# Small values gathered into one tile, turned values put into free places, and two quarters of a K chunk kept, in a decode kernel of four layers

## The chip, the cores and the metric

The kernel runs on one core of one Trainium2 chip. The metric is device time in microseconds of one launch. Three runs of the kernel before gave 673.77, 673.06 and 672.82 us; the median, 673.06, is the time before.

## The reference

Attention with a cache of 4096 positions and an MLP with GELU stand in turn, two of each, for one token of 512 values:

```python
def _A_ref(x, k_cache, v_cache, wq, wo):
    q = (x @ wq).reshape(B, Sq, H, Dh).transpose(0, 2, 1, 3)      # H = 32, Dh = 128
    scores = jnp.einsum("bhqd,bhkd->bhqk", q, k_cache) * (Dh ** -0.5)   # 4096 keys
    p = _softmax(scores, axis=-1)
    o = jnp.einsum("bhqk,bhkd->bhqd", p, v_cache)
    return o.transpose(0, 2, 1, 3).reshape(B, Sq, H * Dh) @ wo
def _B_ref(x, w1, b1, w2, b2):                                    # 512 -> 1376 -> 512
    return jnp.einsum("bsf,fd->bsd", _gelu(jnp.einsum("bsd,df->bsf", x, w1) + b1), w2) + b2

x = A_x
x = x + _A_ref(_layernorm(x), A_k_cache, A_v_cache, A_wq, A_wo)
x = x + _B_ref(_layernorm(x), B_w1, B_b1, B_w2, B_b2)
x = x + _A_ref(_layernorm(x), A_k_cache, A_v_cache, A_wq, A_wo)   # the same caches and weights
x = x + _B_ref(_layernorm(x), B_w1, B_b1, B_w2, B_b2)
```

All values are float32. One pass over the caches and weights is some 157 MB, far over what the core's memory holds.

## The kernel before

**Two passes.** A pass is one attention layer and its MLP. The 32 heads are taken in eight groups of four. A group's K is one block of 128 partitions by 32 quarters of 512 values (a quarter, `U`, is 256 KB; four are a chunk, 32 a block of 8 MB); its V has the same size. Pass one takes the groups from 0 to 7, pass two from 7 back to 0, so that what the first leaves in the memory serves the second: K of group 7 whole, V of group 7 whole, V of group 6 in part (26 quarters in place and six copied into PSUM tiles `pK`), and of K of group 6 one quarter, copied by ScalarE into `KEPT_K` (line 399).

**The arena.** One large tile holds a ring of three homes of a block each (`A_AT`, `B_AT`, `C_AT`), and behind the third home, from `SHARED` on, places for the MLP's weights, one quarter of scratch (`SCRATCH`), and a `PAIR` of weight blocks, wo of this group and wq of the next. Beside the arena there are tiles of their own: the identity for transposes, `zq` (queries with zeros around them), `x_wide` and `on_wide` (operands of 128 columns and a few more, of which a matmul reads a window), the biases, `ml` and `mb` of the softmax, a tile `smalls` of 160 columns for all small values, and two work buffers, `turned` and `mt`, for transposed values.

**A group.** `scores` multiplies K by a query that stands in a window of `zq`; `exponentials` finds the maximum, turns it into a bias with two small transposes on VectorE (DVE) and lets ScalarE take the exponentials; `weights` transposes them on TensorE (PE) into PSUM `pO` and copies them into a `turned` buffer, and forms the reciprocal sum `rl`. Of V, PE multiplies three chunks of eight; DVE multiplies the other five by the weights and adds them up (`weighted`, lines 239 to 250). These sums and the group's output product come only in the next group, beside its scores (`group`, lines 369 to 381): `sum_up`, `head` (which writes `on_wide`), the scores, `out_product` with windows of `on_wide`, `exponentials`, the turn of the output by four transposes of DVE, and `weights`. The next group's queries are made with windows of `x_wide` (`next_queries`).

**What sets the order.** All loads of weights, K and V go out on one queue (SP, SyncE), in program order; a load whose place is still being read makes all behind it wait. The first input `xcol` and the biases go out on ScalarE's queue. PE's matmuls are kept in program order. Other instructions are ordered by a scheduler at compile time, which also makes every wait from the places that instructions read and write.

**The change of passes** (lines 415 to 484). After the last V chunks come wo, w1 in four loads, and w2 in five (`W2_AT_CHANGE`), each into the places of w1 that have just been read. Behind w2 come wq for the second head group of pass two (when row 3 of w2 is through), K of group 6 in pieces (`begin_k`), into places that become free one after another, and a pair of weight blocks. Meanwhile PE takes the scores of group 7 from K that is there (line 456), its exponentials, the queries of group 6 (line 465), the weights and V of group 7 (line 469). When these values are through, the next K block may be loaded into `A_AT`. `idle` is a matmul with zero weights whose result nobody uses; it fills PE's waits.

Of the kernel before, what the change touches and what calls it, by code (L numbers as in the profile page):

```python
# [22 lines left out]
J = 4  # L23
# [30 lines left out]
def decode_layers(ctx: ExitStack, tc: tile.TileContext, x, k, v, w, w1, b1, w2, b2, out):  # L54
    nc = tc.nc
    const = ctx.enter_context(tc.tile_pool(name="const", bufs=1))
    work = ctx.enter_context(tc.tile_pool(name="work", bufs=1))
# [5 lines left out]
    smalls, places = ctile("smalls", 160), {}  # L63

    def small(name, n=1):
        if name not in places:
            a = sum(b - a for a, b in places.values())
            places[name] = a, a + n
        a, b = places[name]
        assert b <= 160 and b - a == n  # L70
        return smalls[:, a:b]

# [29 lines left out]
    nc.scalar.dma_start(xcol, x)  # L102
    nc.scalar.dma_start(b1c, b1)
    nc.scalar.dma_start(b2c, b2)

    ident = ctile("ident", P)
    make_identity(nc, ident)
    negmean = ctile("negmean", 32)
    nc.vector.memset(negmean, -1.0 / D)
    power = small("power")  # L110
    nc.gpsimd.memset(power, -0.5)

    zero, one = small("zero", 4), small("one")
    nc.vector.memset(zero, 0.0)
    nc.vector.memset(one, 1.0)
# [5 lines left out]
    for t in (pS, pO):  # L121
        nc.vector.memset(t, 0.0)
    zq = ctile("zq", J, 2 * C - 1)
    ml, mb = (ctile(n, 32) for n in ("ml", "mb"))
    for t in (zq, ml, mb):
        nc.vector.memset(t, 0.0)

    def of_32(t, n, i=0):
        return t[:, : 32 * n].rearrange("p (c q) -> p c q", q=32)[:, :, i]


    x_wide, on_wide = ctile("x_wide", 32 * J + 6), ctile("on_wide", 32 * J + 3)
    nc.vector.memset(x_wide, 1.0)
    nc.vector.memset(on_wide, 0.0)

# [5 lines left out]

    def turned(src, wide=False):

        t = work.tile([P, P], F32, name="turned")
        if wide:
            for j in range(J):
                q = slice(32 * j, 32 * j + 32)
                nc.vector.transpose(t[q], src[q, P * j : P * (j + 1)])  # L148
        else:
            nc.vector.transpose(t, src[:, :P])  # L150
        return t
# [16 lines left out]
    def minus_mean(s, at):  # L168
        for j in range(J):
            matmul(at[32 * j : 32 * j + 32, :], negmean, s, start=True, stop=True)  # L170
        return at
# [21 lines left out]

    def queries(to, negm, wide=False):
        qt = turned(to, wide)
        z = zq
        nc.vector.scalar_tensor_tensor(z[:, :, C - 1], of_32(qt, J, 1), negm, of_32(qt, J),
                                       op0=ALU.mult, op1=ALU.add)
        return z

    def scores(z, c, kt):
        for j in range(J):
            matmul(pS[32 * j : 32 * j + C, :], z[:, j, C - 1 - c : 2 * C - 1 - c], kt[j],
                   start=(c == 0), stop=(c == C - 1))

    def exponentials(sc, nsc):
        nc.vector.tensor_reduce(ml[:, 0:1], pS, axis=AX.X, op=ALU.max)  # L207
        mt, m, bias = work.tile([P, 32], F32, name="mt"), small("m"), work.tile([P, 32], F32, name="mt")
        nc.vector.transpose(mt, ml)
        nc.vector.tensor_reduce(m, mt[:, :C], axis=AX.X, op=ALU.max)  # L210
        nc.vector.tensor_scalar(mb[:, :C], m.to_broadcast([P, C]), nsc, None, op0=ALU.mult)
        nc.vector.transpose(bias, mb)  # L212
        p = at(SCRATCH, U)
        nc.scalar.activation(p, pS, AF.Exp, bias=bias[:, 0:1], scale=sc, accum_out=ml[:, 0:1])  # L214
        return p

    def weights(p):
        for b in range(4):
            tc.keep_in_program_order(nc.tensor.transpose(  # L219
                pT[:, b].rearrange("p j r -> p (j r)"), p[:, P * b : P * (b + 1)], ident))  # L220
        pt = work.tile([P, P], F32, name="turned").rearrange("p (c j b) -> p c j b", j=J, c=C)
        nc.vector.tensor_copy(pt, pT[:, :, :, :C].rearrange("p b j c -> p c j b"))  # L222
        lt, l, lr, rl = work.tile([P, 32], F32, name="mt"), small("l"), work.tile([P, 32], F32, name="mt"), small("rl")
        nc.vector.transpose(lt, ml)  # L224
        nc.vector.tensor_reduce(l, lt[:, :C], axis=AX.X, op=ALU.add)
        lb = small("lb", 32)
# [42 lines left out]

    def head_out(rl, wt, last=False):  # L270
        on = head(rl, last)
        to = pS if last else pO
        out_product(on, wt, to, last)
        return of_32(turned(to, wide=not last), 4)

# [9 lines left out]
    def mlp(xs, s, w1_t, w2_t, load_w2=None, behind_w2=None):  # L285
# [107 lines left out]
    for g in range(G):  # L393
# [4 lines left out]
        if g == G - 2:  # L398
            nc.scalar.copy(at(KEPT_K, U), at(k_home + NC * C - U, U))
        if g < G - 2:  # L400
# [14 lines left out]
        if final:  # L415
            wo_t = by_four(load(PAIR, of_w(g % 2, g, 1)))
            for i in range(3):
                load_w1(SHARED, i, i + 1)
            own = head_out(rl, wo_t, last=True)
            load_w1(SHARED, 3, 4)  # L420
        else:
# [3 lines left out]
            z = next_queries(xs, negm, wq_t)  # L425
    x1, s1 = set_x(own, 1.0, acc, queries=False)

    k_t = []
# [125 lines left out]
```

## Time and profile before

| what | value |
|---|---|
| median of three runs | 673.06 us (672.82 to 673.77) |
| the profiled execution's own time | 673.26 us |
| its span from the first to the last instruction | 671.5 us |
| PE, DVE, ScalarE busy, share of the span | 59%, 49%, 3% |
| read from device memory | 285.88 MB, 426 GB/s over the span |
| share of the 16 DMA engines' time, SP's queue | 99.1% |

Rows of the timeline have the start and the length in microseconds, the engine, the line, the operation and its operands (out<-in) with partitions and elements, and how often it came; in brackets stands how long the engine was idle before it and what ended that. SPq and ACTq are the issues of transfers. PEclk, in the busy time by stretches, is the share of TensorE's clock that was granted. Rows of DMA issues give the size in KB and the microseconds from the issue until all has landed; several issues in one row share a median.

### The profile page before, as it was taken

The page shows a single profiled execution, that of the slowest core. Times are in us where ns is not written, and L with a number is a line of the kernel's source. Part 1 is how long each engine was busy: PE and PEld are TensorE (multiplying, and loading weights), DVE is VectorE, ACT ScalarE, POOL GpSimd, SP SyncE. Part 2 cuts the span into 40 slices and gives each one's busy share as a digit, 9 for nine tenths or more (in the row PEclk, how much of TensorE's full clock was granted, in tenths as well). Part 3 has the DMA queues.
Part 4 walks back from the last instruction along what each step waited for, and adds up shares of the span by engine and source line. Part 5 has one row for each costly group of instructions (what it writes and reads, how often), then busy time and mean ns, then how long its engine had stood idle before and what let it go on. Part 6 is the DMA issues. An engine that isn't in the chain of part 4 may idle for free. (4 is left out here: it accounts for less than half of the span.)

```text
span 671.5 us, 5755 instructions
## 1 busy us (share of the span) xinstructions
PE 397.1 (59%) x2458; PEld 107.2 (16%) x2458; DVE 330.9 (49%) x483; ACT 22.5 (3%) x48; POOL 4.4 (1%) x21
## 2 busy tenths in 40 slices
PE   4443753647618456386877878747527466275585
PEld 1100110111202111011213222211102111021122
DVE  2049276393682845930112221294682945927631
ACT  0010000000000000001000110000000000000000
POOL 1000000000000000000000000000000000000000
PEclk9666775976868767677978898978668857687698
DMA  9999999999999999999999999999999999999997
GB/s 375 437 438 434 437 434 437 402 466 437 437 434 401 430 439 437 437 438 423 429 412 403 431 427 432 418 451 438 434 437 409 459 433 427 433 437 413 431 421 299
DMA packets 11545, 286.25 MB, mean 426 GB/s; under 512 B 1792, under 2 KB 1792, under 8 KB 3584
## 3 DMA queue, kind: packets, MB, share of 16 engines
q1 hardware_dynamic: 11088, 285.88, 99.1%
q8 instruction: 19, 0.31, 0.2%
q10 hardware_dynamic: 432, 0.01, 0.0%
q14 instruction: 6, 0.05, 0.0%
HBM read 285.88 MB, written 0.00 MB: 426 GB/s over the span
## 5 line engine op out<-in xcount | busy, mean ns | idle before, releaser
L84 PE MATMUL pS<-arena,zq 128*8 128x512 f32 x1024 | 137.3, 697 | 35.2 <-DMA arena<-in_k 31.4
L243 DVE TENSOR_TENSOR arena<-arena,turned 128x10240 f32<-128x10240 f32 x11 | 119.1, 10826 | 41.8 <-DMA arena<-in_v 41.8
L84 PE MATMUL pO<-arena,turned 128*4 128x512 f32 x584 | 98.1, 832 | 53.5 <-DMA arena<-in_v 51.9
L84 PE MATMUL pO<-arena,smalls 128*4 128x512 f32 (+3 forms) x158 | 30.4, 813 | 133.3 <-DVE arena L248 128.0
L248 DVE TENSOR_TENSOR arena<-arena 128x2048 f32<-128x2048 f32 (+1 forms) x33 | 98.5, 2985 | 0.7
L207 DVE TENSOR_REDUCE ml<-pS 128x1 f32<-128x512 f32 x16 | 11.1, 692 | 152.1 <-PE pS L84 152.1
L84 PEld LDWEIGHTS pS<-arena,zq 128*8 128x8 f32 x1024 | 29.3, 100 | 149.6 <-issue 112.7
L84 PE MATMUL pO<-arena,on_wide 128*128 128x512 f32 (+1 forms) x136 | 49.2, 527 | 4.0 <-DVE on_wide L266 2.7
L84 PE MATMUL pS<-arena,x_wide 128*128 128x512 f32 x88 | 41.0, 608 | 2.4 <-DMA arena<-in_w 2.4
L258 DVE STREAM_TRANSPOSE arena<-pO 128x512 f32<-128x512 f32 x16 | 11.5, 717 | 58.2 <-PE pO L84 58.2
L84 PEld LDWEIGHTS pO<-arena,turned 128*4 128x4 f32 x584 | 16.6, 104 | 119.2 <-issue 115.3
L214 ACT ACTIVATE arena<-pS,mt,smalls 128x512 f32<-128x512 f32 x16 | 12.4, 777 | 493.3 <-DVE mt L212 493.3
L219 PE MATMUL pO<-ident,arena 128*128 128x128 f32 x64 | 10.6, 291 | 30.5 <-DVE turned L148 16.4
L148 DVE STREAM_TRANSPOSE turned<-pO 32x128 f32<-32x128 f32 x64 | 19.8, 309 | 17.8 <-PE pO L84 17.1
L84 PEld LDWEIGHTS pO<-arena,smalls 128*4 128x4 f32 (+2 forms) x158 | 3.1, 88 | 145.1 <-DVE arena L248 137.1
L84 PEld LDWEIGHTS pO<-arena,on_wide 128*128 128x128 f32 (+1 forms) x136 | 19.4, 164 | 34.9 <-issue 28.1
L84 PE MATMUL pO<-arena,x_wide 128*2 128x128 f32 (+1 forms) x88 | 16.2, 396 | 9.6 <-POOL x_wide L162 6.7
L84 PEld LDWEIGHTS pS<-arena,x_wide 128*128 128x128 f32 x88 | 16.1, 193 | 32.6 <-DMA arena<-in_w 16.9
L84 PE MATMUL pS<-arena,smalls 128*1 128x128 f32 (+1 forms) x188 | 14.3, 316 | 2.3 <-DVE smalls L309 1.2
L148 DVE STREAM_TRANSPOSE turned<-pS 32x128 f32<-32x128 f32 x44 | 13.7, 311 | 0.8
L219 PEld LDWEIGHTS pO<-ident,arena 128*128 128x128 f32 x64 | 7.0, 145 | 43.2 <-issue 25.1
L224 DVE STREAM_TRANSPOSE mt<-ml 128x32 f32<-128x32 f32 x16 | 3.4, 212 | 17.0 <-ACT arena L214 17.0
(73 smaller groups left out, 95.6 us busy)
## 6 DMA issues: line engine op xcount, KB each, us to landing
arena<-in_w SPq DMA_DIRECT2D x13, 2048.0 KB, 11.5
arena<-in_k SPq DMA_DIRECT2D x4, 4096.0 KB, 25.3
arena<-in_v SPq DMA_DIRECT2D x2, 4096.0 KB, 39.1
arena<-in_w SPq DMA_DIRECT2D x6, 1024.0 KB, 20.4
arena<-in_v SPq DMA_DIRECT2D x3, 2048.0 KB, 43.3
arena<-in_v SPq DMA_DIRECT2D x1, 6144.0 KB, 29.6
arena<-in_w SPq DMA_DIRECT2D x6, 688.0 KB, 30.6
arena<-in_v SPq DMA_DIRECT2D x4, 1024.0 KB, 46.4
```

The source lines that it names most:

```text
L84: tc.keep_in_program_order(nc.tensor.matmul(*a, **kw))
L148: nc.vector.transpose(t[q], src[q, P * j : P * (j + 1)])
L207: nc.vector.tensor_reduce(ml[:, 0:1], pS, axis=AX.X, op=ALU.max)
L214: nc.scalar.activation(p, pS, AF.Exp, bias=bias[:, 0:1], scale=sc, accum_out=ml[:, 0:1])
L219: tc.keep_in_program_order(nc.tensor.transpose(pT[:, b].rearrange("p j r -> p (j r)"), p[:, P * b : P * (b + 1)], ident))
L224: nc.vector.transpose(lt, ml)
L243: nc.vector.tensor_tensor(t, t, w.unsqueeze(2).to_broadcast([P, 4 * J * (C - BY_PE), P]), op=ALU.mult)
L248: nc.vector.tensor_tensor(a, a, b, op=ALU.add)
L258: nc.vector.transpose(ot, pO)
```

## The change

- All tiles beside the arena become columns of one tile, `cells`: the identity, `zq` (39 columns instead of 60, the four heads' windows overlapping in their zeros), one wide operand in place of two (x in columns 0 to 7 of each 32, the head's output in columns 8 to 11), `ml` and `mb` one column apart, and the values of the GELU, which share columns with `lb` and `mt`. Other small values take the 20 columns that are left free in each 32 of the wide operand, in the order in which they are first asked for: negmean, power, one, the values of the mean and the variance, sc, nsc, the maximum `m` and `l` fill the first; `rl`, `o`, `acc` and `x1` the second. Those that come by DMA (xcol and the two biases) lie behind, outside the wide operand, in columns that DVE fills with zeros first; these two memsets now stand ahead of the three transfers.
- `turned` values have no buffer of their own. They go to a free quarter of the arena (`TURNED`), to `SCRATCH` around the change of passes, once to the identity's place (which is rebuilt by `make_identity` after the first queries of pass two) and once into the home `C_AT`.
- `KEPT_K` holds two quarters; ScalarE's copy moves 1024 columns, and the last piece of K of group 6 is 12 quarters instead of 13.
- The second and third load of w2 at the change are rows 2 to 4 and 4 to 8 instead of 2 to 5 and 5 to 8, and the filler matmul behind row 4 stands behind row 3.
- In the first group of pass two a filler matmul is put behind the scores; the queries of group 6 are multiplied ahead of `exponentials`, and turned between its bias and its ScalarE instruction.
- negmean is one column read with stride 0. The scratch for descriptors is 128 instead of 256 bytes per partition.

```diff
+TURNED = SHARED + 9 * U
-ARENA = KEPT_K + U
+ARENA = KEPT_K + 2 * U
+ZQ = C - 1 + J * C
+WIDE = 32 * J + 8 + 3 + 1
+CELLS = 425
-W2_AT_CHANGE = ((0, 2), (2, 5), (5, 8), (8, 10), (10, 11))
+W2_AT_CHANGE = ((0, 2), (2, 4), (4, 8), (8, 10), (10, 11))
...
+    cells = ctile("cells", CELLS)
+    ident, zq, wide = cells[:, :P], cells[:, P : P + ZQ], cells[:, P + ZQ : P + ZQ + WIDE]
+    x_wide, on_wide = wide, wide[:, 8:]
+    first_small = P + ZQ + WIDE
+    by_dma = ("b1c", "b2c", "xcol")
+    gaps, places = [P + ZQ + 32 * j + 12 for j in range(J)], {}
+    ends = [a + 20 for a in gaps]
...
+            fit = [j for j in range(J) if name not in by_dma and gaps[j] + n <= ends[j]]
...
     wq_t = by_four(load(SHARED, of_w(1, 0, 1)))
-    b1c, b2c = ctile("b1c", FB), ctile("b2c", 4)
-    xcol = ctile("xcol", 4)
+    nc.vector.memset(wide, 1.0)
+    nc.vector.memset(cells[:, first_small:], 0.0)
+    b1c, b2c, xcol = small("b1c", FB), small("b2c", 4), small("xcol", 4)
     nc.scalar.dma_start(xcol, x)
...
+    turned_at = [at(TURNED, P)]
...
-        t = work.tile([P, P], F32, name="turned")
+        t = turned_at[0] if to is None else to
...
-    def exponentials(sc, nsc):
+    def exponentials(sc, nsc, between=None):
...
         nc.vector.transpose(bias, mb)
+        if between:
+            between()
         p = at(SCRATCH, U)
...
-                if c in (4, 7, FB - 1):
-                    idle(pO, U if c == 4 else U // 2)
+                if c in (3, 7, FB - 1):
+                    idle(pO, U if c == 3 else U // 2)
...
-            nc.scalar.copy(at(KEPT_K, U), at(k_home + NC * C - U, U))
+            nc.scalar.copy(at(KEPT_K, 2 * U), at(k_home + NC * C - 2 * U, 2 * U))
...
-            own = head_out(rl, wo_t, last=True)
+            own = head_out(rl, wo_t, last=True, home=ident)
...
+    turned_at[0] = at(SCRATCH, P)
...
     negm, z, sc, nsc = first_queries(xs, s, wq_t)
+    make_identity(nc, ident)
...
-            begin_k(C_AT + 2 * NC, 13)
-            k_t.append(at(KEPT_K, U))
+            begin_k(C_AT + 2 * NC, 12)
+            k_t += [at(KEPT_K, U), at(KEPT_K + U, U)]
     pair = load(C_AT + 24 * U, of_w(g % 2, g - 1, 2))
-    p = exponentials(sc, nsc)
+    idle(pO)
     for c in range(4):
         query_block(c, xs, wq_t)
-    z = queries(pO, negm)
+    p = exponentials(sc, nsc, lambda: queries(pO, negm, to=at(C_AT + 21 * U, P)))
     pt, rl = weights(p)
...
+    turned_at[0] = at(TURNED, P)
```

More of the change, by code (lines that the diff above doesn't have):

```diff
@@ L61, in ctile @@
         return const.tile([P, *shape], F32, name=name)
-    smalls, places = ctile("smalls", 160), {}
+    cells = ctile("cells", CELLS)
+    ident, zq, wide = cells[:, :P], cells[:, P : P + ZQ], cells[:, P + ZQ : P + ZQ + WIDE]
+    x_wide, on_wide = wide, wide[:, 8:]
+    first_small = P + ZQ + WIDE
+    ml, mb = cells[:, first_small : first_small + 32], cells[:, first_small + 1 : first_small + 33]
+    gelu = first_small + 33
+    lb, mt = cells[:, gelu : gelu + 32], cells[:, gelu + 32 : gelu + 64]
+    rest = gelu + 6 * FB
+    by_dma = ("b1c", "b2c", "xcol")
+    gaps, places = [P + ZQ + 32 * j + 12 for j in range(J)], {}
+    ends = [a + 20 for a in gaps]
     def small(name, n=1):
+        nonlocal rest
+        if name.startswith("gelu_"):
+            i = "huaztg".index(name[-1])
+            return cells[:, gelu + FB * i : gelu + FB * (i + 1)]
         if name not in places:
[L67 to L71, printed above, removed]
+            fit = [j for j in range(J) if name not in by_dma and gaps[j] + n <= ends[j]]
+            if fit:
+                places[name] = gaps[fit[0]], n
+                gaps[fit[0]] += n
+            else:
+                places[name] = rest, n
+                rest += n
+        a, m = places[name]
+        assert m == n and rest <= CELLS
+        return cells[:, a : a + n]
     arena = const.tile([P, ARENA], F32, name="arena")
@@ L104, in decode_layers @@
     nc.scalar.dma_start(b2c, b2)
-    ident = ctile("ident", P)
     make_identity(nc, ident)
-    negmean = ctile("negmean", 32)
+    negmean = small("negmean")
     nc.vector.memset(negmean, -1.0 / D)
@@ L111, in decode_layers @@
     nc.gpsimd.memset(power, -0.5)
-    zero, one = small("zero", 4), small("one")
-    nc.vector.memset(zero, 0.0)
+    one = small("one")
     nc.vector.memset(one, 1.0)
@@ L122, in decode_layers @@
         nc.vector.memset(t, 0.0)
[L123 to L126, printed above, removed]
+    nc.vector.memset(zq, 0.0)
+    zero = zq[:, :4]
+    turned_at = [at(TURNED, P)]
     def of_32(t, n, i=0):
         return t[:, : 32 * n].rearrange("p (c q) -> p c q", q=32)[:, :, i]
-    x_wide, on_wide = ctile("x_wide", 32 * J + 6), ctile("on_wide", 32 * J + 3)
-    nc.vector.memset(x_wide, 1.0)
-    nc.vector.memset(on_wide, 0.0)
     def in_quarters(t, n):
@@ L140, in pairs, with turned @@
         return t[:, :8].rearrange("p (c i) -> p c i", i=2)
-    def turned(src, wide=False):
-        t = work.tile([P, P], F32, name="turned")
+    def turned(src, wide=False, to=None):
+        t = turned_at[0] if to is None else to
         if wide:
@@ L169, in minus_mean @@
         for j in range(J):
-            matmul(at[32 * j : 32 * j + 32, :], negmean, s, start=True, stop=True)
+            matmul(at[32 * j : 32 * j + 32, :], negmean.to_broadcast([P, 32]), s, start=True, stop=True)
         return at
@@ L202, in scores @@
         for j in range(J):
-            matmul(pS[32 * j : 32 * j + C, :], z[:, j, C - 1 - c : 2 * C - 1 - c], kt[j],
+            matmul(pS[32 * j : 32 * j + C, :], z[:, C * j + C - 1 - c : C * j + 2 * C - 1 - c], kt[j],
                    start=(c == 0), stop=(c == C - 1))
-    def exponentials(sc, nsc):
+    def exponentials(sc, nsc, between=None):
         nc.vector.tensor_reduce(ml[:, 0:1], pS, axis=AX.X, op=ALU.max)
-        mt, m, bias = work.tile([P, 32], F32, name="mt"), small("m"), work.tile([P, 32], F32, name="mt")
+        m, bias = small("m"), mt
         nc.vector.transpose(mt, ml)
@@ L273, in head_out @@
         out_product(on, wt, to, last)
-        return of_32(turned(to, wide=not last), 4)
+        return of_32(turned(to, not last, home), 4)
     def out_product(on, wt, to, narrow=False):
```

16 lines of the change are left out of this document (7 added, 9 removed).

## The prediction

> **What bounds the kernel now.** First the page's busy times, slices and queues.
>
> ```profile
> PE 397.1 (59%) x2458; PEld 107.2 (16%) x2458; DVE 330.9 (49%) x483; ACT 22.5 (3%) x48; POOL 4.4 (1%) x21
> ...
> GB/s 375 437 438 434 437 434 437 402 466 437 437 434 401 430 439 437 437 438 423 429 412 403 431 427 432 418 451 438 434 437 409 459 433 427 433 437 413 431 421 299
> q1 hardware_dynamic: 11088, 285.88, 99.1%
> ```
>
> The slices stand at 434 to 438 GB/s wherever the loads are large, and the transfers of SP's queue alone fill 99.1% of the DMA engines' time, while PE is busy for 59% of the span and DVE for 49%. So bytes set the time, as long as each load is issued before the queue runs dry; at the end the last load is followed by a short tail. I therefore price the change in bytes, and for each other edit I ask whether it makes a load late or lengthens that tail.
>
> How early is early enough? At the change of passes two cases show it (start and length of the issue, and by the groups of DMA issues, KB and us from issue to landing; the four landings belong to the four issues in order).
>
> ```profile
> 361.76 0.33 SPq L80 DMA_DIRECT2D arena<-in_w  x1
> 364.55 0.33 SPq L80 DMA_DIRECT2D arena<-in_w  x1
> 377.65 0.33 SPq L80 DMA_DIRECT2D arena<-in_w  x1
> 390.02 0.33 SPq L80 DMA_DIRECT2D arena<-in_k  x1
> ...
> arena<-in_w SPq DMA_DIRECT2D x1, 256.0 KB, 5.1
> arena<-in_w SPq DMA_DIRECT2D x1, 1024.0 KB, 5.8
> arena<-in_w SPq DMA_DIRECT2D x1, 2048.0 KB, 17.2
> arena<-in_k SPq DMA_DIRECT2D x1, 24.3
> ```
>
> The 256 KB load lands at 361.76 + 5.1 = 366.9. The next one, of 1024 KB, is issued 2.3 us before that and lands at 370.35, 3.5 us later, where its bytes at 437 GB/s take 2.4: 1.1 us are lost. The K load of 8192 KB is issued at 390.02, 4.8 us before the pair ahead of it lands (377.65 + 17.2 = 394.85), and lands at 414.3, 19.5 us later against 19.2 for its bytes: hardly a loss. So a lead under about 2.3 + 1.1 = 3.4 us loses the difference; I use that below.
>
> **The change, part by part.** *The kept quarter.* One K load shrinks from 13 quarters to 12.
>
> ```profile
> arena<-in_k SPq DMA_DIRECT2D x1, 3328.0 KB, 14.1
> ```
>
> A quarter is 3328 / 13 = 256 KB, and at 437 GB/s that is 0.60 us. ScalarE's copy doubles:
>
> ```profile
> L399 ACT COPY arena<-arena x1: 618/618/618, 287.9 to 287.9; 128x512 f32<-128x512 f32 x1
> 299.01 0.78 ACT L214 ACTIVATE arena<-pS,mt,smalls 128x512 f32<-128x512 f32 x1 [10.46 <-DVE mt L212]
> ```
>
> It takes 0.62 to 1.24 us in place of 0.62, inside the 10.46 us in which ScalarE waits anyway: nothing. Uncovered it would cost at most 0.62.
>
> *W2's pieces.* 1024 + 512 KB (rows 2..4 and 4..8 in another cut) stand for two times 768 KB: the same bytes in the same number of transfers, each waiting for the same w1 chunk. Nothing, give or take 0.1. The filler matmul moves from row 4 to row 3; the load behind row 3 is the one issued at 364.55, and it needs row 3's matmuls in both versions.
>
> *The identity, overwritten and rebuilt.* These are two more POOL instructions (0.2 us each at the mean of the 21 above). They stand behind the first queries of the second pass, before the scores; the transposes that need the identity come at 380.33, 8.7 us after the load issued behind the first scores at 371.64 (rows below), and POOL has nothing else: nothing, 0.4 if the transposes had to wait.
>
> *Without a price.* The mean's matmuls read negmean with stride 0, as the operands one and zero are already read; zq is closed up; the DMA scratch is halved, and no load goes through POOL. The numbers of instructions stay.
>
> *The start.* xcol now lies in a tile that DVE has first to fill, with two memsets ahead of its transfer.
>
> ```profile
> 0.73 0.41 ACTq L102 DMA_DIRECT2D xcol<-in_x  x1
> 0.81 0.09 DVE L109 MEMSET negmean<- 128x32 f32 x1 [0.81 <-PEq L543]
> 1.16 0.42 SPq L80 DMA_DIRECT2D arena<-in_k  x1
> 1.17 0.46 ACTq L103 DMA_DIRECT2D b1c<-in_b  x1
> 2.22 0.17 DVE L133 MEMSET x_wide<- 128x134 f32 x1
> 13.54 0.33 SPq L80 DMA_DIRECT2D arena<-in_v  x1
> ...
> arena<-in_w SPq DMA_DIRECT2D x1, 1024.0 KB, 5.0
> xcol<-in_x ACTq DMA_DIRECT2D x1, 2.0 KB, 5.2
> arena<-in_k SPq DMA_DIRECT2D x1, 23.9
> b1c<-in_b ACTq DMA_DIRECT2D x1, 5.5 KB, 24.1
> ```
>
> DVE starts at 0.81, two memsets of about 0.17 end at 1.15, so xcol is issued near 1.18, just behind K's 1.16 instead of 0.43 ahead of it. b1c shows what that means: issued 0.01 us after K, it landed only with K. Its 128 rows, 8 for each of 16 engines, went out one by one between K's rows, each of which takes (23.9 - 5) / 8, about 2.4 us. xcol so far went between rows of the first weights (1024 KB, 0.30 us a row) and landed with them at 5.9. A start 0.45 us later loses 0.45 / 0.30 = 1.5 turns, 2 in whole turns; if K's rows are also set up first (0.42), 0.87 / 0.30 = 2.9, so 3. Each lost turn comes 2.4 us later. I take 2; bounds 0 and, if all 8 go behind K's rows, 8. The V load at 13.54 waits for the first queries and these for x; I add 0.5 because the second half of them now reads columns that the mean's small values share. It moves to 13.54 + 0.5 + 4.8 = 18.8, and needs to be out 3.4 us before K's landing (1.16 + 23.9 = 25.1), by 21.7. Nothing; 3 turns (21.2) still nothing; 4 are a rival below.
>
> [...]
>
> *Small values inside the wide operand.* The running maximum m now lies in columns that on_wide's matmuls read, so DVE may write it only when they are through. In the loop (start, length):
>
> ```profile
> 78.95 3.70 PE L84 MATMUL pO<-arena,on_wide 128*128 128x512 f32 x8
> 80.07 0.16 DVE L210 TENSOR_REDUCE smalls<-mt 128x1 f32<-128x8 f32 x1
> 80.84 0.78 ACT L214 ACTIVATE arena<-pS,mt,smalls 128x512 f32<-128x512 f32 x1 [42.52 <-DVE mt L212]
> 82.72 1.27 DVE L148 STREAM_TRANSPOSE turned<-pO 32x128 f32<-32x128 f32 x4
> 84.14 0.63 PE L219 MATMUL pO<-ident,arena 128*128 128x128 f32 x4 [1.49 <-DVE turned L148]
> 89.41 10.83 DVE L243 TENSOR_TENSOR arena<-arena,turned 128x10240 f32<-128x10240 f32 x1 [4.32 <-DMA arena<-in_v]
> ```
>
> m moves from 80.07 to about 82.7, and the exponentials with it to 83.5. But the transposes already waited for the four turns that follow the same matmuls. If m's three steps (80.84 - 80.07 = 0.8) go first, the turns and all behind them are 0.7 late; if the turns go first, 1.6. Queued behind them are the transposes and the weights, then the V products, which wait 4.32 us for V in this group. Nothing in the loop; DVE's chain and the next loads start from V's landing. In the last group of the second pass V is there already; the values, and PE after them, slip by 0.7:
>
> ```profile
> 658.29 1.33 PE L84 MATMUL pO<-arena,smalls 128*2 128x344 f32 x8 [2.21 <-DMA arena<-in_w]
> ```
>
> There 2.21 us of waiting for w1 cover it; without cover it is 0.7 to 1.6. The tail after the last load stays.
>
> *The change of passes.* A filler matmul now stands ahead of the second head group's queries, and it reads the first quarter of a place into which K is being loaded.
>
> ```profile
> 371.64 0.33 SPq L80 DMA_DIRECT2D arena<-in_k  x1
> arena<-in_k SPq DMA_DIRECT2D x1, 1024.0 KB, 7.8
> ...
> 352.17 1.12 PE L84 MATMUL pS<-arena,smalls 128*128 128x512 f32 x2
> 377.41 1.06 PE L84 MATMUL pO<-arena,x_wide 128*2 128x128 f32 x32
> 377.92 1.07 ACT L476 COPY arena<-pK 128x512 f32<-128x512 f32 x2 [15.25 <-PE pO L84]
> 379.40 0.78 ACT L214 ACTIVATE arena<-pS,mt,smalls 128x512 f32<-128x512 f32 x1 [0.41 <-DVE mt L212]
> 380.33 0.66 PE L219 MATMUL pO<-ident,arena 128*128 128x128 f32 x4 [1.86 <-ACT arena L214]
> 381.40 8.55 PE L84 MATMUL pO<-arena,turned 128*4 128x512 f32 x64 [0.42 <-DVE turned L222]
> ...
> 380.00:384.00 4.00, 3.25 (x20) 0.91 (x24) 1.01 (x6) 0.27 (x2) 0.00 (x0) 0.63 1.06 455
> ```
>
> That K piece lands at 371.64 + 7.8 = 379.4. PE waits for it, then filler 1.12, queries 1.06, turn 0.32 (a quarter of the 1.27 above) with 0.2 of handing over: the transposes come at 382.1 instead of 380.33, the values at 383.2 instead of 381.40. The values took 8.55 us. A granted clock of 0.63 over the four us from 380 means half clock for (1 - 0.63) x 2 x 4 = 3.0 us of them, so from 381.0 on: they lost 2.6 / 2 = 1.3 us and need 7.25 at full clock. Started at 383.2 they lose 0.4 to the same slow stretch and end at 390.85; with queries and transposes partly slowed, 391.1, which I take. Bounds: 390.45 with no slow stretch, 392.1 with a whole one (3.0 us at half clock, 1.5 lost, and 0.15 in handing over). The K load behind the values goes out then. The pair ahead of it now lands at 394.85 - 0.60 = 394.25: a lead of 3.15, a loss of 0.25 (0 to 1.25). The next load, of V at 399, is issued while that K load of 19 us still runs, so a microsecond there costs nothing.
>
> [...]
>
> **The sum**: -0.60 + 0.25 = -0.35 us. The profiled execution took 673.26 (span 671.5 and 1.8 around it), 0.2 above the median of 673.06; that gives 672.9 for it, and 672.7 as a median. The likeliest range is 672.3 to 673.3. A measurement here can tell 0.2%, 1.35 us, from no change, so I expect no change that it can tell.
>
> **The rivals.** *The K load falls behind at the change*: ScalarE keeps its two copies ahead of the exponentials as at 377.92; these need the queries' end, 381.6, so exponentials start at 382.7, values at 384.7 (all 3.3 later than in the rows), and end at 391.95: lead 2.3, loss 1.1, 673.06 - 0.60 + 1.1 = 673.6 as a median, and with a whole slow stretch (1.5) 675.1; I write 674.2. For it speaks the order before; against it, that the copies are ready later than the bias now.
>
> *Slower: x too late.* Four lost turns put the V load at 13.54 + 0.5 + 9.6 = 23.6, a lead of 1.4 us and a loss of 2.0: 674.7, and 2.4 more for each further turn. It decides from the fourth turn, an issue of xcol about 1.0 us later than before. For it: the b1c row; against it: the memsets end near 1.15.
>
> *Faster*: the 1.1 us lost ahead of the load issued at 364.55 close as W2's second piece lands sooner: 671.6. Against it: that load waits for row 3's matmuls, and these for the activation, not for W2.
>
> *The copy saves nothing*: the queue still carries 285.88 MB, 673.1; the two edits of the load's length and of its list of places speak against it.
>
> **How the numbers follow.** My forecast 0.62; K load late 0.17; x late 0.10; gap closed 0.06; nothing saved 0.05. Faster by over 0.2% (under 671.7): the gap's 0.06 and some chance from unknown clocks, 0.08. Slower (over 674.4): x late nearly whole and a third of the K case, 0.15. Same: 0.77. For 8 in 10 the range takes in the gap and most of the K case: 671.5 to 674.5.
>
> **What would show it.** The queue's bytes 285.62 MB; a K load of 3072 KB; xcol landing near 10.7 and the V load issued near 18.8, before 21.7; on_wide's matmuls ending before m is written, with V still awaited by DVE; the transposes at the change near 382 and the K load near 391. An xcol landing after 15, a K load after 392.1, or DMA slices that fall at 25 us or at 392 us would make it wrong.

## The result, and the profile after

The changed kernel takes **676.65 us** (median of 6 runs, 676.22 to 679.50), the kernel before beside it on the same chip 673.8 us (672.82 to 674.19): a ratio of 1.0051, with a 95% interval of 1.0038 to 1.0064. It is slower by about 2.9 us. The forecast was 672.7 with a range up to 674.5; the time lies above it, on the side to which the forecast gave 0.15. The profiled execution took 676.51 us, its span is 674.7. Ratios, here and below, leave out an execution over 1.5% above the fastest of its kernel, which concerns one of e9 and one of e10.

The page after, its slices and its main queue:

```profile
PE 397.6 (59%) x2460; PEld 107.8 (16%) x2460; DVE 329.1 (49%) x480; ACT 22.9 (3%) x48; POOL 4.9 (1%) x23
...
GB/s 373 435 435 432 435 437 435 408 456 435 435 431 411 457 432 436 435 432 405 429 411 380 425 403 433 415 459 432 428 435 411 457 435 428 428 435 417 433 411 293
q1 hardware_dynamic: 11088, 285.61, 98.9%
```

The bytes fell as intended (285.88 to 285.61 MB), in the same number of packets, and the engines are as busy as before. But the level of the slices in which only large loads run went from 437 to 435 GB/s. These are rounded figures, some half a per cent apart; the landings of single loads, below, give 0.3%. Since it holds in slices all over the span, it is the larger part of the loss.

The second part is local. These are rows of the change of passes in the timeline (PE, and the issues of SP's queue), with two rows by stretches, and the landings of the last two of these loads (KB and us from the issue; the last is the K load):

```profile
381.44 3.73 PE L108 MATMUL pO<-arena,cells 128*128 128x512 f32 x34 [2.47 <-DMA arena<-in_k]
385.71 0.63 PE L240 MATMUL pO<-cells,arena 128*128 128x128 f32 x4 [0.54 <-DVE arena L169]
386.72 7.05 PE L108 MATMUL pO<-arena 128*4 128x512 f32 x64 [0.38 <-DVE arena L243]
379.02 0.33 SPq L104 DMA_DIRECT2D arena<-in_w  x1
393.83 0.33 SPq L104 DMA_DIRECT2D arena<-in_k  x1
381.50:385.00 3.50, 3.50 (x34) 1.38 (x34) 0.93 (x5) 1.03 (x4) 0.00 (x0) 0.51 1.08 463
385.00:389.00 4.00, 3.08 (x36) 1.07 (x32) 0.84 (x3) 0.17 (x1) 0.00 (x0) 1.00 1.03 444
...
arena<-in_w SPq DMA_DIRECT2D x1, 2048.0 KB, 17.0
arena<-in_k SPq DMA_DIRECT2D x1, 23.1
```

PE waits 2.47 us for the K piece into which the filler reads. Filler and queries then run at a granted clock of 0.51 and take 3.73 us, and the K load goes out at 393.83. The pair ahead of it lands at 379.02 + 17.0 = 396.0, so its lead is 2.2 us, and it lands at 393.83 + 23.1 = 416.9, 20.9 later; the 8 MB took 19.5 at this place before. Here 1.4 us are lost.

The start (issues and us to landing) and the last V group of pass two:

```profile
1.17 0.38 ACTq L127 DMA_DIRECT2D cells<-in_x  x1
1.18 0.42 SPq L104 DMA_DIRECT2D arena<-in_k  x1
19.52 0.33 SPq L104 DMA_DIRECT2D arena<-in_v  x1
...
cells<-in_x ACTq DMA_DIRECT2D x1, 2.0 KB, 9.2
...
648.37 0.66 PE L240 MATMUL pO<-cells,arena 128*128 128x128 f32 x4 [2.13 <-ACT arena L235]
649.60 5.33 PE L108 MATMUL pO<-arena 128*4 128x512 f32 x48 [0.57 <-DVE arena L243]
661.34 0.76 PE L108 MATMUL pO<-arena,cells 128*2 128x344 f32 x8 [1.15 <-DMA arena<-in_w]
```

x landed at 1.17 + 9.2 = 10.4, the V load went out at 19.52, over 5 us ahead of K's landing. At the end PE still waits 1.15 us for w1, so the later `m` is covered. Neither explains the loss in this execution.

### The profile page after: what moved, and what is told of

Its sections match the earlier page's. It is cut to its first block, busy times and chain, and to the rows that moved or that the text cites. A ratio compares the mean times of both kernels' runs of the same rounds, so it can differ in the third digit from the quotient of the medians.

```text
span 674.7 us, 5776 instructions
## 1 busy us (share of the span) xinstructions
PE 397.6 (59%) x2460; PEld 107.8 (16%) x2460; DVE 329.1 (49%) x480; ACT 22.9 (3%) x48; POOL 4.9 (1%) x23
## 3 DMA queue, kind: packets, MB, share of 16 engines
q1 hardware_dynamic: 11088, 285.61, 98.9%
HBM read 285.62 MB, written 0.00 MB: 423 GB/s over the span
## 4 chain that ended last, share of the span: by engine, by line
DMA 59%; PE 30%; DVE 9%; issue 1%; another core or an unknown queue 1%; SPq 0%; ACT 0%; POOL 0%; DVEq 0%; ACTq 0%
DMA arena<-in_k 37%; DMA arena<-in_v 16%; PE pS L108 16%; PE pO L108 13%; DMA arena<-in_w 4%; DVE arena L263 3%; DVE arena L268 3%; DMA cells<-in_x 1%; DVE arena L167 1%; SPq L104 0%; DVE cells L229 0%; PE pO L240 0%; ACT arena L235 0%; DVE arena L278 0%
## 5 line engine op out<-in xcount | busy, mean ns | idle before, releaser
L108 PE MATMUL pS<-arena,cells 128*8 128x512 f32 (+2 forms) x1364 | 192.5, 612 | 34.3 <-DMA arena<-in_k 25.4
L108 PE MATMUL pO<-arena,cells 128*128 128x512 f32 (+5 forms) x384 | 98.7, 624 | 155.5 <-DVE arena L268 128.8
L263 DVE TENSOR_TENSOR arena<-arena 128x10240 f32<-128x10240 f32 x11 | 119.1, 10825 | 34.5 <-DMA arena<-in_v 30.3
L108 PE MATMUL pO<-arena 128*4 128x512 f32 x584 | 96.1, 816 | 47.9 <-DMA arena<-in_v 46.2
L108 PEld LDWEIGHTS pS<-arena,cells 128*8 128x8 f32 (+2 forms) x1364 | 52.5, 103 | 188.4 <-issue 140.6
L108 PEld LDWEIGHTS pO<-arena,cells 128*128 128x128 f32 (+3 forms) x384 | 29.8, 127 | 208.1 <-DVE arena L268 137.9
L108 PEld LDWEIGHTS pO<-arena 128*4 128x4 f32 x584 | 16.4, 103 | 112.4 <-issue 108.7
L235 ACT ACTIVATE arena<-pS,cells 128x512 f32<-128x512 f32 x16 | 12.4, 777 | 517.5 <-DVE cells L231 517.5
L167 DVE STREAM_TRANSPOSE arena<-pO 32x128 f32<-32x128 f32 x64 | 19.9, 311 | 20.1 <-PE pO L108 19.1
L167 DVE STREAM_TRANSPOSE arena<-pS 32x128 f32<-32x128 f32 x44 | 13.7, 311 | 0.8
```

Source lines behind the costliest of these rows:

```text
L108: tc.keep_in_program_order(nc.tensor.matmul(*a, **kw))
L263: nc.vector.tensor_tensor(t, t, w.unsqueeze(2).to_broadcast([P, 4 * J * (C - BY_PE), P]), op=ALU.mult)
```

## The experiments

### First round: the two losses at the change

e1 is the changed kernel again. e2 leaves the filler matmul out:

```diff
-    idle(pO)
     for c in range(4):
```

e3 lets it read a home that is full, and not one into which K is being loaded:

```diff
-    idle(pO)
+    matmul(pO, zero[:, 0:1].to_broadcast([P, P]), at(A_AT, U), start=True, stop=True)
```

e4 cuts w2 as before:

```diff
-W2_AT_CHANGE = ((0, 2), (2, 4), (4, 8), (8, 10), (10, 11))
+W2_AT_CHANGE = ((0, 2), (2, 5), (5, 8), (8, 10), (10, 11))
...
-                if c in (3, 7, FB - 1):
-                    idle(pO, U if c == 3 else U // 2)
+                if c in (4, 7, FB - 1):
+                    idle(pO, U if c == 4 else U // 2)
```

> The changed kernel again, beside the other three on one chip, to have one base for them. Theory A (two local losses at the change of passes: the K load issued 2.2 us ahead of the end of the queue loses about 1.5 us, w2 and wq lose about 1.0 more than before; 0.6 us of bytes are saved): about 2 us slower than the kernel before, ratio 1.003. Rival B (the loss is spread over the whole run, by the exponentials that now wait for the output product or by slower transfers): the same ratio, but the landings of the eight large blocks of each pass, 19.30 us apart before, lie further apart than those of the kernel before on the same chip.

> The filler matmul ahead of the second head group's queries is left out; all else is the changed kernel. Theory A: PE no longer waits for the K piece that lands near 381.4, the transposes come at once behind the exponentials, the values some 4 to 5 us earlier unless the clock halves, the K load is issued with a lead over 4 us and loses nothing: 1.3 to 1.6 us faster than the changed kernel. Rival B: no difference over 0.4 us. A second rival C: the filler keeps the clock full, and without it the values run at half clock for 3 us and the K load gains only 1 us or less.

> The same filler matmul at the same place, but reading a quarter of V that is in the memory (the first home) instead of a place into which K is being loaded. Theory A: it is the wait for the landing that costs, so this gains as much as leaving the filler out, 1.3 to 1.6 us against the changed kernel, give or take 0.3 for the clock. If the work of the filler were the cost (rival D), it would stay as slow as the changed kernel.

> w2's loads in the old cut (rows 2 to 5 and 5 to 8) and the filler behind row 4 again; all else is the changed kernel. Theory A: the load of the third piece is issued when w1's chunk 2 is through in both cuts, but with the longer piece ahead of it the queue holds 0.6 us more, so the 0.3 us lost ahead of it come back and at most 0.7 more ahead of wq: 0.3 to 1.0 us faster than the changed kernel. Rival B: no difference over 0.3 us.

Measured: e1 676.88 us, ratio 1.0041 [1.0029, 1.0053]; e2 676.75, 1.0033 [1.0020, 1.0045]; e3 676.12, 1.0033 [1.0021, 1.0045]; e4 676.92, 1.0035 [1.0023, 1.0047]. The K load after the change in e3 and in e4 (issue, us to landing):

```profile
391.27 0.33 SPq L104 DMA_DIRECT2D arena<-in_k  x1
...
arena<-in_k SPq DMA_DIRECT2D x1, 25.6
```

```profile
392.98 0.33 SPq L104 DMA_DIRECT2D arena<-in_k  x1
...
arena<-in_k SPq DMA_DIRECT2D x1, 23.4
```

In e3 the K load takes 25.6 us to its landing, and for the first 6.3 of them the pair ahead is still on its way; it lands 19.3 us behind the pair, so its loss is gone. In e2's trace it is gone too (a lead of 6.3 us). In e4 it isn't (a lead of 2.4, landing 21.0 behind the pair). The mechanism at this load is as read, but e2 and e3 are at most 0.8 us below e1, where 1.3 to 1.6 were expected, e4 gains nothing, where 0.3 to 1.0 were expected, and the intervals of the four overlap. None of these edits undoes most of the loss.

### Second round: both undone, and what else the change moved

e5 is one execution of the kernel before, for its trace on the same chip as e6 to e8. e6 has the edits of e3 and e4 together. e7 is e6 with `m` outside the wide operand, e8 is e6 with the three small transfers in a tile of their own, sent ahead of the memsets:

```diff
-    by_dma = ("b1c", "b2c", "xcol")
+    by_dma = ("b1c", "b2c", "xcol", "m")
```

```diff
+    by_queue = ctile("by_queue", FB + 8)
+    b1c, b2c, xcol = by_queue[:, :FB], by_queue[:, FB : FB + 4], by_queue[:, FB + 4 :]
     nc.scalar.dma_start(xcol, x)
...
+    nc.vector.memset(wide, 1.0)
+    nc.vector.memset(cells[:, first_small:], 0.0)
```

> The kernel before itself, profiled on the chip of these runs, so that landings are compared within one chip. If the chip's transfers are slower than in the trace of before, the large blocks land 19.36 us apart here too instead of 19.30, and 150 MB are moved some 0.7 us later; if the changed kernel itself slows its transfers, they land 19.30 apart.

> The filler at the change reads V that is there, and w2 has its old cut; the rest is the changed kernel. Theory A: the K load loses nothing and w2 and wq lose no more than before, so only the 0.60 us of saved bytes remain: 0.2 to 0.8 us faster than the kernel before. Rival B (a spread loss beside these two): still 0.8 us or more slower than the kernel before.

> As e6, and the running maximum m lies outside the wide operand, so the exponentials need not wait for the output product. My theory: V is awaited in every group of the loop and w1 at the end, so this changes nothing, within 0.3 us of e6. Rival E: the exponentials behind the output product cost time at the end of the second pass: 0.7 to 2 us faster than e6.

> As e6, and the three values that come by DMA have a tile of their own, sent before the memsets as in the kernel before. My theory: xcol lands near 5.9 again instead of 10.3, the V load goes out near 14 instead of 19.5, and the time stays within 0.3 us of e6, because 19.5 was early enough. Rival F: the start costs by crowding the first blocks: 0.5 us or more faster than e6.

Measured: e5 674.2 in its single execution; e6 676.49, 1.0027 [1.0014, 1.0040]; e7 675.84, 1.0027 [1.0017, 1.0037]; e8 676.16, 1.0033 [1.0020, 1.0046]. With both losses undone the kernel is still 0.27% slower than before, so the forecast of e6 (faster by the saved quarter) failed, and its rival of a spread loss held. `m` doesn't show. Of the start e8 says little, since x wasn't late in e6's trace either (it landed at 5.7). One thing was common to every version of the changed kernel, and absent in e5 on the same chip: the 8 MB loads that came in time took a little longer from the landing ahead of them to their own. The middle one of the 23 loads of 8 MB, worked out from issues and landings, took 19.30 us in e5 and 19.30 in the kernel before, and 19.35 to 19.36 in each of the eight traces of the changed kernel (the first one, and e1 to e4, e6 to e8). What these versions share is where the arena lies. In the compiled programs it begins at byte 1024 of each partition before, and at byte 1984 after (1888 in e8), because `cells` ahead of it is longer than `smalls` was and the scratch is halved.

### Third round: the address of the arena

e9 moves the arena back. A tile of 192 columns ahead of it takes the identity, `zq` and what comes by DMA, the rest of `cells` lies behind it; the arena begins at 1024. x still waits for a memset, now the third on DVE:

```diff
-    cells = ctile("cells", CELLS)
-    ident, zq, wide = cells[:, :P], cells[:, P : P + ZQ], cells[:, P + ZQ : P + ZQ + WIDE]
+    head = ctile("head", 192)
+    arena = const.tile([P, ARENA], F32, name="arena")
+    cells = ctile("cells", CELLS)
+    ident, zq, wide = head[:, :P], head[:, P : P + ZQ], cells[:, :WIDE]
...
+    b1c, b2c, xcol = (head[:, a:b] for a, b in ((167, 178), (178, 182), (182, 186)))
...
+    nc.vector.memset(head[:, P + ZQ :], 0.0)
```

e10 is e9 with the edits of e6. e11 and e12 are the reverse test on the kernel before, and differ from each other by 64 bytes of empty columns. In e11 the scratch is halved and the arena stays at 1024, in e12 it begins at 960:

```diff
-    smalls, places = ctile("smalls", 160), {}
+    smalls, places = ctile("smalls", 192), {}     # e12: 176
...
-    nc = bacc.Bacc("TRN2", target_bir_lowering=False, num_devices=1, dynamic_dma_scratch_size=256)
+    nc = bacc.Bacc("TRN2", target_bir_lowering=False, num_devices=1, dynamic_dma_scratch_size=128)
```

> The changed kernel, with one thing moved: ident, zq and the three operands that come by DMA lie in a tile of 192 columns ahead of the arena, the rest of cells behind it, so that the arena starts at byte 1024 of a partition as in the kernel before, and not at 1984. Theory A (the address at which the rows of a load begin is what slows each load by 0.05 to 0.06 us): the 8 MB blocks land 19.30 us apart again, not 19.36; some 2.4 us of the loss go, the time is 0.4 us over the kernel before (ratio 1.0006): 0.6 saved by the kept quarter, 1.0 lost at the change of passes. Theory B (the halved scratch space of the DMAs, or the one tile itself): the spacing stays 19.36 and the ratio 1.004. Theory C (some local loss not yet seen): spacing 19.36 or 19.30, ratio 1.004.

> e9 with both local edits of e6 too (filler matmul reads the last ring slot that came, W2 cut (2,5),(5,8) as before). Theory A: 0.6 us under the kernel before (ratio 0.9991), blocks 19.30 apart. Theory B and C: as e6, ratio 1.0027.

> The kernel before with the scratch space of the DMAs at 128 as in the changed kernel, and 192 columns of smalls so that the arena stays at byte 1024. Theory A and C: no change (ratio 1.000, within 0.001), blocks 19.30 apart. Theory B: blocks 19.36 apart, 2 us slower (ratio 1.003).

> e11 with 176 columns of smalls: the arena starts at byte 960, 64 bytes off. Theory A: blocks 19.36 apart, 2.4 us slower than e11 (ratio 1.0035 to the kernel before). Theory B: as e11, 1.003. Theory C: no change, 1.000.

Measured: e11 673.99 us, 0.9991 [0.9981, 1.0001]; e12 676.96, 1.0038 [1.0027, 1.0048]. **64 bytes cost the old kernel 3.0 us.** The halved scratch by itself shows no cost. In the traces, DVE starts on each V block of pass one as it lands; one group of 8 + 8 + 2 MB lies between two of these rows (first e11, then e12):

```profile
89.62 10.82 DVE L243 TENSOR_TENSOR arena<-arena,turned 128x10240 f32<-128x10240 f32 x1 [4.06 <-DMA arena<-in_v]
133.06 10.83 DVE L243 TENSOR_TENSOR arena<-arena,turned 128x10240 f32<-128x10240 f32 x1 [3.59 <-DMA arena<-in_v]
176.58 10.83 DVE L243 TENSOR_TENSOR arena<-arena,turned 128x10240 f32<-128x10240 f32 x1 [4.86 <-DMA arena<-in_v]
220.37 10.83 DVE L243 TENSOR_TENSOR arena<-arena,turned 128x10240 f32<-128x10240 f32 x1 [4.57 <-DMA arena<-in_v]
```

```profile
90.01 10.83 DVE L243 TENSOR_TENSOR arena<-arena,turned 128x10240 f32<-128x10240 f32 x1 [4.10 <-DMA arena<-in_v]
133.61 10.82 DVE L243 TENSOR_TENSOR arena<-arena,turned 128x10240 f32<-128x10240 f32 x1 [3.72 <-DMA arena<-in_v]
177.21 10.82 DVE L243 TENSOR_TENSOR arena<-arena,turned 128x10240 f32<-128x10240 f32 x1 [3.33 <-DMA arena<-in_v]
220.80 10.83 DVE L243 TENSOR_TENSOR arena<-arena,turned 128x10240 f32<-128x10240 f32 x1 [4.64 <-DMA arena<-in_v]
```

A group takes 43.44, 43.52 and 43.79 us in e11; in e12 it takes 43.60, 43.60 and 43.59. A group now and then is longer in either (the next ones take 43.55 in e11 and 43.98 in e12), so it is the shortest ones that compare: none is under 43.58 where the arena isn't at 1024. The changed kernel has the step of e12:

```profile
133.81 10.82 DVE L263 TENSOR_TENSOR arena<-arena 128x10240 f32<-128x10240 f32 x1 [3.21 <-DMA arena<-in_v]
177.40 10.82 DVE L263 TENSOR_TENSOR arena<-arena 128x10240 f32<-128x10240 f32 x1 [2.54 <-DMA arena<-in_v]
220.99 10.83 DVE L263 TENSOR_TENSOR arena<-arena 128x10240 f32<-128x10240 f32 x1 [2.42 <-DMA arena<-in_v]
```

Two times 43.59. A group is 18.9 MB, the queue carries 285.6 MB, so 15.1 groups' worth; at 0.16 us each (43.60 against 43.44) these are 2.4 us.

The landings of all 8 MB loads leave less to chance. The middle one of 23 is 19.30 us behind the landing ahead of it in e11 and 19.36 in e12. It is 19.30 to 19.32 in each of the seven traces with the arena at 1024 (before, e5, e9, e10, e11, e13, e14), and 19.35 to 19.37 in each of the eleven with the arena elsewhere. The queue carries 34 times 8 MB, at 0.06 us each 2.0. The traces also record every row that was moved: of the rows of 64 KB, 97% took 2.418 us in e11, but a fifth in e12, where half took 2.420 or more and a quarter 2.424 or more. The times of all rows of SP's queue, added up and divided by 16 engines, are 665.8 us in e11 and 667.8 in e12. So 2.0 of the 3.0 us are rows that take longer.

e9 came to 675.62 us, 1.0018 [1.0001, 1.0034], e10 to 674.79, 1.0009 [0.9989, 1.0030]. Both lie below their counterparts e1 and e6, and their 8 MB loads land 19.30 us apart. They aren't as far down as expected (1.0006 and 0.9991, which the intervals still hold), and their runs are spread widely (up to 685.99 and 683.87). The profile of e10, an execution of 683.87 us, shows one reason for the spread (issues, and us from issue to landing):

```profile
1.16 0.42 SPq L104 DMA_DIRECT2D arena<-in_k  x1
1.19 0.39 ACTq L127 DMA_DIRECT2D head<-in_x  x1
32.52 0.33 SPq L104 DMA_DIRECT2D arena<-in_v  x1
...
arena<-in_k SPq DMA_DIRECT2D x1, 23.8
head<-in_x ACTq DMA_DIRECT2D x1, 2.0 KB, 23.9
arena<-in_v SPq DMA_DIRECT2D x1, 22.1
```

x, 0.03 us behind K, landed with K at 25.1; the V load went out at 32.52, 7.6 us after the queue had run dry. It is the rival "x too late", with all eight turns lost: x's 128 rows left in eight groups of 16, some 2.4 us apart, as the prediction had it. In e7 the profiled execution, of 677.72 us, had lost four; its V load went out 1.0 us ahead of K's landing at 25.4 and lost 2.1 us, near the prediction's price of 2.0:

```profile
24.43 0.33 SPq L104 DMA_DIRECT2D arena<-in_v  x1
...
cells<-in_x ACTq DMA_DIRECT2D x1, 2.0 KB, 14.1
```

### Fourth round: everything put back, one by one

e13 is e10, and e14 is e9, without the memset that x waits for. e15 and e16 are the kernel before at two other addresses: 896 (scratch halved, 160 columns) and 1056 (scratch as before, 168 columns).

```diff
-    nc.vector.memset(head[:, P + ZQ :], 0.0)
```

> e10 without the memset ahead of the three small transfers, so that x is issued with the first weights as in the kernel before: arena at byte 1024, W2 cut as before, filler reads a slot that is full, x in time. Theory A (address, change of passes and late x are all there is): x lands at about 5.8 us in every execution, no execution above 676; 0.6 us saved by the kept quarter, ratio 0.9991. Rival D (the kept quarter's 0.6 us are given back at another place, most likely ahead of the last weights): ratio 1.000 and the last load lands as long after its issue as before.

> e9 without that memset: address and start are as before, W2 cut and filler as in the changed kernel. Theory A: 1.0 us above e13 (ratio 1.0006), the K chunk issued behind the change with less than 3 us in the queue ahead of it and landing 20 us or more behind the pair ahead. Rival D: as e13 plus the same 1.0 us.

> The kernel before with the scratch space at 128, smalls of 160 columns: the arena starts at byte 896, which is 128 bytes off a multiple of 256. If rows must begin at multiples of 256 bytes: as e12, ratio 1.0038, blocks 19.36 apart. If 64 bytes or 128 are the bound: no change, ratio 0.9991, blocks 19.30 apart.

> The kernel before with 168 columns of smalls: the arena starts at byte 1056, 32 bytes off. If only the start off a multiple counts: as e12, ratio 1.0038, blocks 19.36 apart. [...] If rows must begin at multiples of 64 at the least: 1.004 or more.

Measured: e13 673.63 us, 0.9991 [0.9980, 1.0002]; e14 674.66, 1.0009 [0.9997, 1.0021]; e15 676.24, 1.0032 [1.0021, 1.0042]; e16 677.28, 1.0046 [1.0032, 1.0060].

e13 is 0.67 us under the kernel before: that fits the 0.60 of the kept quarter, though the interval still holds no change. One of its twelve executions took 676.39, where none above 676 was expected; why isn't known. e14, which differs from e13 by the filler's place and w2's cut, is 1.0 us above it, with overlapping intervals. Where time goes is in the traces. First e13, then e14 (the second and third load of w2, the pair, and the K load; issues, KB and us to landing):

```profile
357.70 2.03 SPq L104 DMA_DIRECT2D arena<-in_w  x2
379.15 0.33 SPq L104 DMA_DIRECT2D arena<-in_w  x1
390.18 0.33 SPq L104 DMA_DIRECT2D arena<-in_k  x1
...
arena<-in_w SPq DMA_DIRECT2D x2, 768.0 KB, 5.7
arena<-in_w SPq DMA_DIRECT2D x1, 2048.0 KB, 16.7
arena<-in_k SPq DMA_DIRECT2D x1, 24.9
```

```profile
357.46 2.03 SPq L104 DMA_DIRECT2D arena<-in_w  x2
377.87 0.33 SPq L104 DMA_DIRECT2D arena<-in_w  x1
392.31 0.33 SPq L104 DMA_DIRECT2D arena<-in_k  x1
...
arena<-in_w SPq DMA_DIRECT2D x1, 1024.0 KB, 6.5
arena<-in_w SPq DMA_DIRECT2D x1, 512.0 KB, 5.0
arena<-in_w SPq DMA_DIRECT2D x1, 2048.0 KB, 17.8
arena<-in_k SPq DMA_DIRECT2D x1, 23.3
```

With the new cut, the 512 KB land at 357.46 + 5.0 = 362.5. The 1024 KB behind them are issued at 357.46 + 2.03 - 0.33 = 359.2, a lead of 3.3 us, and land at 365.7, 3.2 later, where their bytes at 437 GB/s take 2.4: 0.8 are lost there. With the old cut the two landings are 1.8 apart, what 768 KB need. But these 0.8 us are made good before the pair lands: from the issue of the first of these loads to the landing of the pair it is 38.2 us in e13 (357.70 to 395.9) and 38.2 in e14 (357.46 to 395.7). In e13 the loads between lose the same time elsewhere. Behind the pair the two differ: the K load of e14 lands at 415.6, 19.9 after it, that of e13 at 415.1, 19.2 after it. These 0.7 us are about what the spans of the two traces differ by (673.4 and 672.6 us). So in these two executions the filler's place costs, and w2's cut doesn't.

e15 lies 128 bytes off a multiple of 256 and pays like e12 (676.24 and 676.96 us), so in this kernel it isn't enough to begin at a multiple of 64 (960) or 128 (896). e16, 32 bytes off, pays at least as much (677.28; its 8 MB loads land 19.37 us apart), so the cost doesn't grow with the bytes by which the start is off. Every run without this cost had the arena at 1024; whether 256, 512 or 1024 is the bound was not measured. The cost depends on the place that is written, since e11 and e12 differ in that alone, and it is a step from 19.30 to 19.36 us for each 8 MB load, 0.3%. By what mechanism the start costs, no trace shows.

## Why the prediction was wrong

**The step that failed is "Without a price".** It put the halved scratch at nothing, on the ground that the numbers of instructions stay, and it had no term at all for where the arena comes to lie when the tiles ahead of it change their length. It counted instructions and bytes, and never asked at which byte the rows of a load begin. The kernel's time is bytes by the rate of the DMA engines, as the first part of the prediction said (SP's queue fills 98.9% of their time in the page after), so what changes that rate by 0.3% is worth 2 us. e11 against e12 prices it: 3.0 us in the old kernel. In the changed kernel, e6 and e13 differ by the address and by x's start, and the ratio falls from 1.0027 to 0.9991, some 2.4 us. No rival had it.

**The kept quarter** was right: 285.61 MB against a forecast of 285.62, and 3072 KB. The 0.67 us of e13 fit the 0.60, within an interval that also holds no change.

**The change of passes** had the right mechanism and the wrong size: 0.25 us by the working, with bounds of 0 to 1.25. In the trace after, it is 1.4, or 1.7 against the 19.2 of the bytes. The lead was 2.2 where 3.15 was forecast. The K piece for which the filler waits came at 381.4 and not at 379.4, but the pair came later by nearly as much (396.0, forecast 394.25), so this took only 0.2 of the lead. The rest is PE's: filler and queries took 3.73 us at a granted clock of 0.51, where 1.12 + 1.06 stood in the sum, and the values, 7.05 at a clock of 1.00 instead of 7.9, won back half of that; they began at 386.72 where 383.2 was forecast. The price of a lead was too low as well: by the prediction's estimate of 3.4 us, worked out from two loads, a lead of 2.2 costs 1.2, and it cost 1.7. At this one K load, leads of 2.2 to 2.7 lost 1.7 to 1.9 us (after, e4, e1), 3.4 lost 0.7 (e14), 4.8 lost 0.3 (before), and 5.7 and 6.3 next to nothing (e13, e2, e3). For the smaller loads ahead the lead alone doesn't decide: 3.3 lost 0.1 in e3, 0.4 in the trace after and 0.8 in e14, and 3.9 lost nothing in e13 and 0.7 in e6. The loss ahead of the load behind row 3, which the rival "Faster" saw closing, stayed: 1.7 us in the trace after, 1.1 before.

The filler didn't keep the clock up in the trace after: PE stood still for 2.47 us ahead of it, and the granted clock was 0.51 from 381.5 to 385.0. With the filler at a home that is full, PE's longest wait between the scores and the values is 0.91 us in e3, e6 and e13, and in e13 the clock is at 1.00 there:

```profile
381.50:385.00 3.50, 2.55 (x24) 0.96 (x28) 1.25 (x8) 0.92 (x3) 0.00 (x0) 1.00 1.04 449
```

Without a filler, waits of 1.86 us (before) and 1.95 us (e2) were followed by a slow stretch too: the granted clock was 0.63 from 380 to 384 in the kernel before, and 12 matmuls of the values took 2.74 us in e2, where 28 took 3.19 in e13. The length of one wait doesn't settle it: the 2.13 us ahead of 648.37 in the trace after were followed by a clock of 1.00 from 649.6 to 654.9. In the rival "K load falls behind" the place was right, and its price of 1.1 to 1.5 near the measured 1.4.

**W2's pieces** at "nothing, give or take 0.1" isn't refuted. The third load's lead falls from 3.9 in e13 to 3.3 in e14, and 0.8 are lost there, which I hadn't looked for; but they are made good before the pair lands, and e4, with the old cut in the changed kernel, takes 676.92 against 676.88 of e1 (the ratios, 1.0035 and 1.0041, leave a few tenths of a microsecond open). How the 1.0 us between e13 and e14 divide over filler and w2 was not measured with both free of the rest.

**The start** came as forecast in the profiled execution: two turns, x at 10.4 (10.7 forecast), V's issue at 19.5 (18.8), nothing lost. That it was two turns is in part luck, since this is no fixed number. In the traces of versions where x goes out behind a memset it lost no turn (e1, e3, e4, e6, e9), two (after, e2), four (e7) and all eight (e10); x took 4.7 us to its landing in e1, 9.2 in the trace after, 14.1 in e7 and 23.9 in e10. A chance of 0.10 for the rival treated the kernel as having one start; it has one in each execution. What it costs in the median isn't settled: e9 and e14 differ by it alone, 675.62 and 674.66, on two chips, and their intervals overlap. No execution of e13 and e14, where x goes out first, took over 677.5; single ones of e9 and e10 took 679 to 686.

**The small values in the wide operand** were right: `m` waits for the output product, the exponentials and the values slip, and PE still waits 1.15 us for w1 behind them (2.21 before). e7, which takes `m` out, has the ratio of e6.

Put together: -0.7 for the quarter (e13), +1.0 for the change of passes (e14 less e13), and +2.6 that are left to the measured +2.9. For the address the landings give 2.0, and e12 less e11 gives 3.0. The sum agrees within what these runs can tell; the part of e12's 3.0 us beyond 2.0 I can't place.

## What to carry to other kernels

Where DMA bytes set the time, look at the byte at which the destination rows begin, whenever a tile ahead of a large buffer changes its length: a shift of 64 bytes cost 3.0 us of 674 here (e11, e12), and DVE's product over a V block took 10.82 to 10.83 us in both. Compare the landings of equal loads between two traces, on the same chip: the constant step of 0.06 us for each 8 MB load was no local wait here, and with both local waits undone (e6) the kernel was still 0.27% slower than before. Let a filler matmul read a place that is full; the one that read a place still being loaded waited itself (2.47 us in the trace after), and the work behind it too. Send a small transfer that the first work needs ahead of the first large load, not next to it: x took 5.1 us to its landing where it went out ahead (e13, e14), and 4.7 to 23.9 where it went out within 0.03 us of K.

## What the runs showed of the hardware that was not expected

- The arena at byte 1024 or at 960, 896 or 1056 of a partition: 673.99, 676.96, 676.24 and 677.28 us for the same kernel. A start on a multiple of 128 wasn't enough (896); which larger multiple is needed was not measured.
- Rows of two queues' transfers that were issued 0.01 to 0.03 us apart didn't pass in a fixed order: x, issued at 1.17 to 1.19, landed after 4.7 us (e1, below; issued 0.01 behind K), after 9.2 (issued 0.01 ahead of K), 14.1 or 23.9 us.

```profile
cells<-in_x ACTq DMA_DIRECT2D x1, 2.0 KB, 4.7
```
